# Seven block products in place of eight in the experts of two batches (attention and two expert layers, one core)

## The chip, the cores and the metric

The kernel runs on one core of a Trainium2 chip. The metric is the device time of one execution in microseconds. Engines: TensorE (PE, with its weight loads PEld), VectorE (DVE), ScalarE (ACT), GpSimd (POOL) and the DMA queues, here issued by SyncE (SP) and ACT.

## What is computed

```
attention: q, k, v of (4, 12, 448, 64)
  q_n, k_n = rmsnorm(q) * g_q, rmsnorm(k) * g_k
  attn = softmax(q_n @ k_n.T / 8);  o = attn @ v
x = o as (1792 tokens, 768)
first experts:   h = x @ w_in (768 x 2048);  g = where(h > 0, h, exp(h) - 1);  y = g @ w_out
second experts:  yn = y / rms(y) * rms_g
  g = yn @ w_gate (768 x 1536);  out = (silu(g) * (yn @ w_val)) @ w_out2
```

All inputs are float32. A product of two float32 matrices is made of three fp32r matmuls: each operand is split in a rounded part (h) and the rest (l), and wh·xh + wh·xl + wl·xh is summed (`mm3`, line 836). So each 128x128 weight tile costs three matmuls of 448 columns for each batch of 448 tokens.

## The kernel before, in words

Tokens lie on the free axis: a tile is 128 features x 448 tokens of one batch. The experts run in five stages (`STAGES`): first experts of batch 0, first experts of batch 1, second experts of batches 0 and 1, first experts of batches 2 and 3, second experts of batches 2 and 3. The attention of 24 head pairs is cut in pieces that are given between the steps of the first three stages; the last pairs end near the end of the third. From then on only the experts run.

First experts go in groups of NF1 = 4 chunks f of the 2048 hidden features: four `h_unit` steps (each output chunk f, for each batch: 6 weight tiles, 18 matmuls, then the ELU on ACT and DVE and the split of g in h and l), then six out steps in `acc_units` (each output chunk e, for each batch: 4 weight tiles, 12 matmuls), added up in the `ybig` tiles. Second experts go alike: four steps of gate and val, then six out2 steps. Here a batch pair makes 24 matmuls in each out step. With the last out group of the first experts each y is scaled and split for the second experts (`y_done`), and its squares are summed for the norm (`norm`), whose factor `rt` is multiplied to each gate product.

Weights are streamed in chunks of six tiles (`w_split`): read, split with `copy` and `tt` into one of 4 buffers of `r_w`, which hold them until TensorE has used them. At their first use they are converted (`w_convert`) and written back to `kept`; from the fourth stage on they are all read from `kept`. The attention outputs of batches 2 and 3 are spilled and read again at the end of the third stage, where `split_x` splits them.

Nothing is issued in the order in which the code is written. `plan.add` collects each operation with the engines that may do it and a price for each, and `Plan.schedule` deals them out in a list schedule with those prices; the earlier written goes first among those ready. `copy` may go to DVE, ACT or POOL (POOL not from a bank), `tt` to DVE or POOL (POOL only if both inputs are in SBUF). In the trace `copy` is on lines 327 to 333, `tt` on line 347 (DVE) and 349 (POOL), `stt` on line 364, `act` on line 372, matmuls on line 304.

```
def tt(dst, a, b, op, eng="vg"):
    ...
        alts["v"] = (c_tt(a, b, n), lambda: V.tensor_tensor(out=dst, in0=a, in1=b, op=op))
    if "g" in eng and two_sbuf(a, b):
        alts["g"] = (0.25 + 0.0022 * n, lambda: G.tensor_tensor(out=dst, in0=a, in1=b, op=op))
```

Of the kernel before, what the change touches and what calls it, by code (L numbers as in the profile page):

```python
# [19 lines left out]
P = 128  # L20
CW = 6
NF1 = 4
NF2 = 4
FIRST = 2
# [3 lines left out]
class Plan:  # L28
# [11 lines left out]
    def __init__(self):  # L40
        self.ops = []
        self.hist = {}
# [31 lines left out]
    def add(self, alts, outs, ins, lag=0.0, after=None, soon=False, dma=False):  # L74
# [3 lines left out]
        for aps, wr in ((ins, False), (outs, True)):  # L78
            for ap in aps:
                if ap is None:  # L80
                    continue
                name, hv, m = self.region(ap)
                h = self.hist.setdefault(name, [])
# [128 lines left out]
def k_tile_order(cd, cf1, cf2):  # L212

    order = []
    for f0 in range(0, cf1, NF1):
        for f in range(f0, f0 + NF1):
            order += [("in", c, f) for c in range(cd)]
        for e in range(cd):
            order += [("out", f, e) for f in range(f0, f0 + NF1)]
    for f0 in range(0, cf2, NF2):  # L220
# [3 lines left out]
        for e in range(cd):  # L224
            order += [("out2", f, e) for f in range(f0, f0 + NF2)]
# [4 lines left out]
def kernel(ctx: ExitStack, tc: tile.TileContext, dims, tok, qk, vr, gq, gk, wst, rmsg, ident_in, out):  # L230
# [8 lines left out]
    T, V, A, G, SP = nc.tensor, nc.vector, nc.scalar, nc.gpsimd, nc.sync  # L239
# [3 lines left out]
    plan = Plan()  # L243
# [174 lines left out]
    tks = [sb.tile([P, 15 * D], F32, name="tk"), wf[:, 0:15 * D]]  # L418
    tks += [yf[:, 7 * S:7 * S + 15 * D], yf[:, 12 * S - 15 * D:12 * S]]
    l_rw = Pair(sb.tile([P, 1024], F32, name="rw"), wf[:, 1024:2048])  # L420
    l_rb = Pair(sb.tile([P, 512], F32, name="rb"), wf[:, 2048:2560])
    l_qh = Pair(sb.tile([P, 1024], F32R, name="qh"), gf[:, 0:1024])
    l_ql = Pair(sb.tile([P, 1024], F32R, name="ql"), gf[:, 1024:2048])
    p_own = sb.tile([P, 3, 2 * S], F32, name="p")
    pt_own = sb.tile([P, 2, 3, S], F32, name="pt")
    l_p = Pair(p_own, tf[:, 0:6 * S].rearrange("p (a s) -> p a s", a=3))
    l_pj = Pair(sb.tile([P, S], F32, name="pj"), tf[:, 6 * S:7 * S])
    l_pt = Pair(pt_own, yf[:, 0:6 * S].rearrange("p (h k s) -> p h k s", h=2, k=3))
    l_pe = Pair(sb.tile([P, S], F32, name="pe"), yf[:, 6 * S:7 * S])
    r_rv = Ring("rv", 2, [P, 512])  # L430
# [7 lines left out]
    r_rsb = Ring("rsb", 2, [P, S])  # L438
    r_xf = Ring("xf", 1, [P, S])
    banks = [pp.tile([P, 512], F32, name=f"bank{k}") for k in range(8)]  # L440
# [13 lines left out]
    stream = [n for kind, _ in STAGES for n in (one if kind == 1 else two)]  # L454
# [7 lines left out]
    uses = {n: stream.count(n) for n in set(stream)}  # L462

    def w_split():
        i = wpos["spl"]
        n = stream[i]
        wpos["spl"] += 1
        if n in kept:
            c = r_wc.next()
            dma(c, kept[n], P * WN * 4)  # L470
        else:
            c = w_convert(n)
        w = r_w.next()
        copy(w[:, 0], c)
        tt(w[:, 1], c, w[:, 0], ALU.subtract)
        if n not in kept and uses[n] > 1:
            kept[n] = tc.dram_tile([P, WN], F32, name=f"kept{n}")
            dma(kept[n], c, P * WN * 4)
        spl_w[i] = w
# [37 lines left out]
    def w_ahead():  # L517
        while wpos["spl"] < min(wpos["i"] // CW + len(r_w.t), len(stream)):
            w_split()

# [358 lines left out]

    def h_unit(f, xs):  # L880
# [16 lines left out]
    def acc_units(bs, f0, nf, first, last, dst, half, done):  # L897
        for e in range(CD):
            w = take_w(nf)
            for b in bs:  # L900
                o = product(w, [gs[f0 + k, b] for k in range(nf)])
                if e == CD - 1:
# [21 lines left out]
    def first_experts(bs):  # L924
        xs = {b: [xT.pop(b * NPB + c) for c in range(CD)] for b in bs}
# [4 lines left out]

        def y_done(e, b, ye):
            g, sq = rg[:, e:e + 1], sqs[b]
            xh, xl = xslots.get(), xslots.get()
            act(xh, ye, AF.Copy, scale=g)
            stt(xl, ye, g, xh, ALU.mult, ALU.subtract)
            xns[b][e] = (xh, xl)
# [4 lines left out]
            yslots.put(ye)  # L941

        for f0 in range(0, CF1, NF1):
            last = f0 + NF1 >= CF1
            for f in range(f0, f0 + NF1):
                h_unit(f, xs)
                yield
            if last:
                for b in bs:
# [42 lines left out]
    def second_experts(bs):  # L992
# [6 lines left out]
        for f0 in range(0, CF2, NF2):  # L999
            last = f0 + NF2 >= CF2  # L1000
            for f in range(f0, f0 + NF2):
                yield from gv_unit(f, bs)
            if last:
                for b in bs:
# [29 lines left out]
    GOALS = [13.25, 19.75, 24, 24, 24]  # L1034
    phase(0)
# [3 lines left out]
    for s, (kind, bs) in enumerate(STAGES):  # L1039
# [13 lines left out]
        for step in first_experts(bs) if kind == 1 else second_experts(bs):  # L1053
# [102 lines left out]
```

## Time and profile before

| | |
|---|---|
| median of 3 runs | 1314.97 us (1314.67 to 1317.63) |
| profiled execution | 1316.42 us, span 1314.6 us |
| mean granted clock | 0.991 |
| TensorE busy | 1266.3 us, 96% of the span |
| POOL, DVE, ACT busy | 756.7, 650.2, 647.1 us |

The span is the time from the first to the last instruction; the execution's own time lies 1.8 us above it. Busy time is an average over stages that have different limits, so the views of single stretches say more than the table. Times of an engine include the time in which an instruction had begun and waited for a port.

### The profile page before, as it was taken

To read this page: it belongs to the slowest core of one execution; us is meant where nothing else is said; L and a number is where in the kernel's file an instruction comes from. 1 tells how busy PE (TensorE), PEld (TensorE's weight loads), DVE (VectorE), ACT (ScalarE), POOL (GpSimd) and SP (SyncE) were. 2 spreads that over 40 slices of the span, in tenths; PEclk is the share of its full clock that TensorE was granted. 3 is DMA by queue.
4 is the path that set the end of the run, shared out by engine and by line. 5 is a ranking of instruction groups with operands and counts; after the bars stand their busy time and mean duration, and the time that the engine had idled before them with its cause. 6 is when DMAs were issued, how large, how long until landed. Compare 5 with 4: busy or idle time off the path is not lost.

```text
span 1314.6 us, 17693 instructions
## 1 busy us (share of the span) xinstructions
PE 1266.3 (96%) x6484; PEld 1062.9 (81%) x6484; DVE 650.2 (49%) x1071; ACT 647.1 (49%) x1263; POOL 756.7 (58%) x576
## 2 busy tenths in 40 slices
PE   4899998988999999999999999999999999999998
PEld 3457766766777777888988889999999999999998
DVE  6787867796444569744564552102121652133332
ACT  5786767776665578555553541433323533221220
POOL 2385677776665588664653673645445765353450
PEclk8999999999999999999999999999999999999999
DMA  6477777665444354654445344111111111111112
GB/s 215 119 233 243 259 250 227 225 226 173 135 131 119 120 191 161 239 162 153 158 153 157 110 137 154 49 60 50 59 48 61 49 61 48 61 49 61 48 37 84
DMA packets 62487, 173.43 MB, mean 132 GB/s; under 512 B 10940, under 2 KB 20160, under 8 KB 62400
## 3 DMA queue, kind: packets, MB, share of 16 engines
q1 hardware_dynamic: 53760, 163.31, 38.3%
q10 hardware_dynamic: 8640, 8.99, 2.4%
q8 instruction: 51, 0.84, 0.3%
q14 instruction: 36, 0.29, 0.1%
HBM read 137.11 MB, written 35.17 MB: 131 GB/s over the span
## 4 chain that ended last, share of the span: by engine, by line
PE 79%; DMA 6%; POOL 5%; DVE 3%; ACT 3%; issue 2%; ACTq 0%; SPq 0%; POOLq 0%; DVEq 0%
PE bank L304 76%; PE bank L317 4%; POOL w L349 1%; DMA tk<-tok 1%; POOL ql L349 1%; DMA wr<-wst 1%; DMA rsum<-rt 1%; DMA rw<-qk 1%; DVE bank L660 1%; DMA wc<-kept 1%; POOL tbig L349 1%; POOL gbig L349 1%; ACT tbig L372 1%; DMA rsb<-rsum 1%; ACT p L372 1%
## 5 line engine op out<-in xcount | busy, mean ns | idle before, releaser
L304 PE MATMUL bank<-xs,w 128*128 128x448 f32 x2880 | 611.7, 369 | 4.3 <-POOL xs L349 2.8
L304 PEld LDWEIGHTS bank<-xs,w 128*128 128x128 f32 x2880 | 536.0, 189 | 55.1 <-issue 7.9
L304 PE MATMUL bank<-gbig,w 128*128 128x448 f32 x2016 | 434.8, 370 | 9.2 <-POOL gbig L349 4.3
L349 POOL TENSOR_TENSOR w<-wc,w 128x768 fp32r<-128x768 f32 x160 | 300.8, 1880 | 202.4 <-ACT w L329 196.0
L304 PEld LDWEIGHTS bank<-gbig,w 128*128 128x128 f32 x2016 | 373.8, 189 | 47.5 <-POOL gbig L349 6.4
L349 POOL TENSOR_TENSOR gbig<-tbig,gbig 128x448 fp32r<-128x448 f32 x107 | 132.0, 1234 | 68.6 <-ACT gbig L329 67.4
L329 ACT ACTIVATE w<-wc 128x768 fp32r<-128x768 f32 x91 | 76.9, 845 | 181.1 <-PE bank L304 173.2
L660 DVE TENSOR_REDUCE bank<-bank 128x1 f32<-128x448 f32 x168 | 98.6, 626 | 50.2 <-PE bank L304 49.4
L349 POOL TENSOR_TENSOR tbig<-tbig 128x448 f32<-128x448 f32 x67 | 85.0, 1269 | 64.7 <-DVE tbig L364 61.9
L364 DVE SCALAR_TENSOR_TENSOR tbig<-tbig,bank 128x448 f32<-128x448 f32 x64 | 39.5, 618 | 161.9 <-ACT tbig L372 161.9
L333 POOL TENSOR_SCALAR w<-wc 128x768 fp32r<-128x768 f32 x77 | 68.5, 890 | 84.0 <-PE bank L304 53.7
L364 DVE SCALAR_TENSOR_TENSOR wc<-wc,wt 128x768 int32<-128x768 int32 x68 | 86.8, 1276 | 29.3 <-ACT wc L495 24.5
L329 ACT ACTIVATE pt<-bank 128x384 f32<-128x384 f32 (+1 forms) x164 | 69.9, 448 | 61.2 <-PE bank L317 52.5
L372 ACT ACTIVATE p<-bank,nm,rr 128x448 f32<-128x448 f32 x126 | 90.2, 720 | 8.6 <-DVE nm L661 6.4
L329 ACT ACTIVATE gbig<-tbig 128x448 fp32r<-128x448 f32 x92 | 53.1, 577 | 78.9 <-DVE tbig L347 48.0
L372 ACT ACTIVATE tbig<-tbig 128x448 f32<-128x448 f32 x112 | 64.5, 576 | 47.4 <-DVE tbig L347 45.0
L347 DVE TENSOR_TENSOR tbig<-bank,tbig 128x448 f32<-128x448 f32 x48 | 29.9, 623 | 102.5 <-PE bank L304 102.3
L317 PE MATMUL bank<-ident,p 128*128 128x128 f32 x441 | 72.4, 280 | 7.8 <-DVE pt L327 3.2
L317 PEld LDWEIGHTS bank<-ident,p 128*128 128x128 f32 x441 | 54.5, 142 | 27.3 <-issue 4.9
L347 DVE TENSOR_TENSOR ybig<-bank,ybig 128x448 f32<-128x448 f32 x72 | 44.5, 620 | 62.2 <-PE bank L304 61.9
L364 DVE SCALAR_TENSOR_TENSOR ybig<-bank,ybig 128x448 f32<-128x448 f32 x48 | 30.0, 624 | 76.1 <-PE bank L304 76.1
L364 DVE SCALAR_TENSOR_TENSOR tbig<-tbig 128x448 f32<-128x448 f32 x48 | 52.9, 1102 | 24.0 <-ACT tbig L372 24.0
(103 smaller groups left out, 1197.5 us busy)
## 6 DMA issues: line engine op xcount, KB each, us to landing
wr<-wst SPq DMA_DIRECT2D x68, 768.0 KB
wc<-kept SPq DMA_DIRECT2D x100, 384.0 KB
kept<-wc SPq DMA_DIRECT2D x68, 384.0 KB
rw<-qk SPq DMA_DIRECT2D x21, 512.0 KB
tk<-tok SPq DMA_DIRECT2D x20, 480.0 KB
rv<-vr SPq DMA_DIRECT2D x24, 256.0 KB
out_t<-ybig SPq DMA_DIRECT2D x24, 224.0 KB
rb<-scr ACTq DMA_DIRECT2D x36, 128.0 KB
```

Source lines behind the costliest of these rows:

```text
L304: T.matmul(o, l, r, start=start, stop=stop)
L317: T.transpose(o, i, ident)
L329: alts["a"] = (c_a(n), lambda: A.activation(out=dst, in_=src, func=AF.Copy))
L333: lambda: G.tensor_scalar(out=dst, in0=src, scalar1=1.0, scalar2=0.0, op0=ALU.mult, op1=ALU.add),
L347: alts["v"] = (c_tt(a, b, n), lambda: V.tensor_tensor(out=dst, in0=a, in1=b, op=op))
L349: alts["g"] = (0.25 + 0.0022 * n, lambda: G.tensor_tensor(out=dst, in0=a, in1=b, op=op))
L364: {"v": (c_tt(a, b, size(dst)), lambda: V.scalar_tensor_tensor(out=dst, in0=a, scalar=s, in1=b, op0=op0, op1=op1))},
L372: {"a": (c_a(size(src)) + extra, lambda: A.activation(out=dst, in_=src, func=func, **kw))},
L660: vop(c_v1(S), lambda mx=mx, ot=o[t]: V.tensor_reduce(out=mx, in_=ot, axis=AX.X, op=ALU.max, negate=True), [mx], [o[t]])
```

## The change

In the last two stages (batches 2 and 3) the products of in, gate and val go by blocks (`quad`). A block has two output chunks f, two batches and the 6 input chunks as two halves of 3: a 2x2 times 2x2 product of blocks, done with seven products of 9 matmuls (`part`) in place of eight, by Strassen's scheme with fifteen sums: four of weights (`w_split`, 128x384 each, S1 to S4), four of inputs (`combo`, T1 to T4, 128x448 each) and seven of products (in `quad`, each with one operand in a bank). Each of the seven weight and seven input combinations is split in h and l. The input combinations of the first experts are made from the spilled tiles at the end of the third stage, those of the second experts in the last out group of the fourth, as soon as y for chunks c and c+3 of both batches is there: for that the out steps go in the order 0, 3, 1, 4, 2, 5 (`E_ORDER`, in all stages). The norm's squares and scale stay, the scale now writes y in place.

Once the attention has ended (`late`), its buffers are used again: as 18 more tiles for the input combinations (42 in all), as two more weight buffers (six chunks ahead instead of four; named `late` in the order), and as two more work tiles. The out products and all of batches 0 and 1 are as before. The core of the diff:

```diff
--- before.py
+++ after.py
+E_ORDER = (0, 3, 1, 4, 2, 5)
...
+    def again(t):
+        f = t if len(t.shape) == 2 else t.rearrange("p a s -> p (a s)") if len(t.shape) == 3 else t.rearrange("p h k s -> p (h k s)")
+        second[t.name] = {"t": None, "shape": list(t.shape), "name": f"late{len(second)}", "tag": t.name.rsplit("_", 1)[0]}
+        return f.bitcast(F32R)
...
+    for t in (p_own, pt_own):
+        f = again(t)
+        wide.append(f[:, 0:2 * WN].rearrange("p (a n) -> p a n", a=2))
+        spare += [f[:, 2 * WN + k * S:2 * WN + (k + 1) * S] for k in range(2)]
+    r_ws = Ring(tiles=[wf[:, k * WN:(k + 1) * WN] for k in range(2)])
+    r_th = Ring(tiles=[wf[:, 2 * WN + k * S:2 * WN + (k + 1) * S] for k in range(3)] + [r_wt.t[0][:, 0:S]])
+    r_more = [r_rsb.t[0], r_xf.t[0]]
...
+            for a, b in duos:
+                res += [("q", j, nums[k + a], nums[k + b]) for j in range(4)]
+            res += [("c", nums[k + nf + j]) for j in range(OG)]
...
+        if j == 0:
+            c0, c1 = w_f32(n0), w_f32(n1)
+            sa, sb = r_ws.next(), r_ws.next()
+            tt(sa[:, 0:HW], c1[:, 0:HW], c1[:, HW:WN], ALU.add)
+            tt(sa[:, HW:WN], sa[:, 0:HW], c0[:, 0:HW], ALU.subtract)
+            tt(sb[:, 0:HW], c0[:, 0:HW], c1[:, 0:HW], ALU.subtract)
+            tt(sb[:, HW:WN], c0[:, HW:WN], sa[:, HW:WN], ALU.subtract)
+            duo["c"] = (c0, sa, sb, c1[:, HW:WN])
+        spl_w[i] = split_w(duo["c"][j], HW if j == 3 else WN)
...
+    def part(w, x):
+        o = r_m.next()[:, 0:S]
+        for k in range(3):
+            mm3(o, w[k], x[k], k == 0, k == 2)
+        return o
+
+    TX = {}
+
+    def quad(eat):
+        w, tx = take_duo(), TX
+        u2, u3, u4, u7 = (r_tp.next() for _ in range(4))
+        p1 = r_tp.next()
+        copy(p1, part(w["A11"], tx["B11"]), "va")
+        p6 = part(w["S2"], tx["T2"])
+        tt(u2, p6, p1, ALU.add)
+        p2 = part(w["A12"], tx["B21"])
+        tt(p2, p2, p1, ALU.add)
+        eat(0, 0, p2)
+        p7 = part(w["S3"], tx["T3"])
+        tt(u3, p7, u2, ALU.add)
+        p5 = part(w["S1"], tx["T1"])
+        tt(u7, p5, u3, ALU.add)
+        tt(u4, p5, u2, ALU.add)
+        eat(1, 1, u7)
+        p4 = part(w["A22"], tx["T4"])
+        tt(p4, u3, p4, ALU.subtract)
+        eat(1, 0, p4)
+        p3 = part(w["S4"], tx["B22"])
+        tt(p3, p3, u4, ALU.add)
+        eat(0, 1, p3)
+        w_ahead()
+
+    def combo(c, x):
+        def sp(name, t):
+            h, l = xslots.get(), xslots.get()
+            copy(h, t)
+            tt(l, t, h, ALU.subtract)
+            TX.setdefault(name, [None] * 3)[c] = (h, l)
+
+        b11, b21, b12, b22 = x
+        t1, t2 = r_tp.next(), r_tp.next()
+        sp("B11", b11)
+        tt(t1, b12, b11, ALU.subtract)
+        tt(t2, b22, t1, ALU.subtract)
+        sp("T2", t2)
+        tt(b12, b22, b12, ALU.subtract)
+        sp("T3", b12)
+        sp("T1", t1)
+        sp("B21", b21)
+        tt(t2, t2, b21, ALU.subtract)
+        sp("T4", t2)
+        sp("B22", b22)
...
+    def h_quad(f, bs):
+        quad(lambda i, j, o: h_eat(f + i, bs[j], o))
...
+        quad(gate)
+        yield
+        quad(val)
+        yield
...
-        for e in range(CD):
+        for e in E_ORDER:
...
+            act(ye, ye, AF.Copy, scale=g)
+            if e >= 3 and b == bs[1]:
+                combo(e - 3, [y[k, bb] for bb in bs for k in (e - 3, e)])
...
+    def late():
+        state["late"] = True
+        for z in spare:
+            xslots.put(z)
+        r_w.t += wide
+        r_tp.t += r_more
...
             if step == "next":
-                if spilled:
-                    until(target(NPAIR) + 1)
-                    for b in ahead[1]:
-                        for i in range(b * NPB, b * NPB + NPB):
-                            xf = r_tp.next()
-                            dma(xf, xT[i], P * S * 4)
-                            split_x(i, xf)
+                if ahead is not None and ahead[0] == 1 and s + 1 in FAST:
+                    if not state:
+                        until(target(NPAIR) + 1)
+                        late()
+                    combos(ahead[1])
                 continue
```

`Engine` (new) hands each operation on to its engine and puts the reused tile in place of the old one; with it all instructions of the changed kernel carry the line 260.

The order of instructions is the same on every engine, but for buffer names, up to the first sum of input tiles in the third stage. From there on TensorE has 180 instructions fewer (6079 for 6259). Two places:

POOL, in the last out group of the first experts of batches 2 and 3 (`tbig` holds work tiles, `w` the split weights; `wc` weights, `wr` their sums, `ybig` y, `xs` and `late` the combinations). Before:

```order
L349 TENSOR_TENSOR w_97<-wc_93,w_97 128x768
L349 TENSOR_TENSOR tbig<-tbig 128x448 x4
L349 TENSOR_TENSOR w_98<-wc_94,w_98 128x768
L349 TENSOR_TENSOR tbig<-tbig 128x448
L333 TENSOR_SCALAR w_99<-wc_92 128x768
```

Now:

```order
L260 TENSOR_TENSOR xf_124<-ybig,rsb_122 128x448
L260 TENSOR_TENSOR xs_69<-rsb_122,xs_68 128x448
L260 TENSOR_TENSOR xs_81<-xf_124,xs_80 128x448
L260 TENSOR_TENSOR late_6535<-ybig,late_6535 128x448
L260 TENSOR_TENSOR w_97<-wc_93,w_97 128x384
L260 TENSOR_TENSOR xs_79<-ybig,xs_78 128x448
L260 TENSOR_TENSOR tbig<-tbig 128x448
L260 TENSOR_TENSOR wr<-wr,wc_94 128x384
L260 TENSOR_TENSOR tbig<-ybig,tbig 128x448
L260 TENSOR_TENSOR xs_83<-tbig,xs_82 128x448
```

Between two weight chunks stood sums of squares; now sums and splits of combinations and sums of weights stand there too, and most weight splits of this stretch have gone to DVE.

DVE, where the norm of these batches ends and the gate products begin (`bank` is PSUM, `gbig` takes the split squares and later g). Before:

```order
L347 TENSOR_TENSOR gbig<-tbig,gbig 128x448 x2
L380 RECIPROCAL tbig<-tbig 128x448
L347 TENSOR_TENSOR tbig<-bank_125,tbig 128x448
L380 RECIPROCAL tbig<-tbig 128x448
L364 SCALAR_TENSOR_TENSOR tbig<-tbig 128x448
L347 TENSOR_TENSOR tbig<-bank_126,tbig 128x448
L347 TENSOR_TENSOR tbig<-tbig,bank_127 128x448
```

Now:

```order
L260 TENSOR_TENSOR tbig<-tbig,ybig 128x448
L260 TENSOR_TENSOR gbig<-tbig,gbig 128x448
L260 TENSOR_TENSOR tbig<-bank_126,tbig 128x448
L260 RECIPROCAL tbig<-tbig 128x448 x2
L260 TENSOR_TENSOR bank_127<-bank_127,tbig 128x448
L260 TENSOR_TENSOR tbig<-bank_128,tbig 128x448
L260 TENSOR_TENSOR tbig<-bank_127,tbig 128x448
L260 TENSOR_TENSOR xf_124<-bank_129,tbig 128x448
L260 TENSOR_TENSOR rsb_122<-bank_129,tbig 128x448
L260 SCALAR_TENSOR_TENSOR wr<-wr,tbig 128x448
```

The two reciprocals stood one gate read apart; now both stand ahead of all but one of the reads of the first block's products, the one of the sixth product, and four of the five bank reads that follow are sums of the scheme.

## Rows read from the trace of the kernel before

**Rows 1.** Page, parts 1 and 2: busy time, and 40 slices of the span.

```profile
PE 1266.3 (96%) x6484; PEld 1062.9 (81%) x6484; DVE 650.2 (49%) x1071; ACT 647.1 (49%) x1263; POOL 756.7 (58%) x576
...
PE   4899998988999999999999999999999999999998
...
PEclk8999999999999999999999999999999999999999
```

**Rows 2.** Chain of waits, its last rows: start, duration (us), engine, tile, instructions.

```profile
773.84 7.30 PE bank L304 x36
781.47 529.64 PE bank L304 x2612
```

**Rows 3.** Windows: stretch, its length, busy us (instructions) of each engine, clock, DMA share.

```profile
core 0: us, PE busy (x) PEld busy (x) DVE busy (x) ACT busy (x) POOL busy (x), PEclk, DMA share, GB/s
200.00:300.00 100.00, 91.58 (x482) 70.15 (x481) 77.98 (x129) 71.71 (x156) 75.71 (x58) 0.97 0.67 223
...
814.00:1050.00 236.00, 236.00 (x1166) 218.70 (x1165) 53.70 (x81) 85.15 (x145) 125.38 (x95) 1.00 0.18 55
1050.00:1311.00 261.00, 261.00 (x1289) 241.66 (x1287) 81.45 (x100) 63.41 (x95) 119.77 (x85) 1.00 0.18 56
1019.70:1048.70 29.00, 29.00 (x145) 26.87 (x144) 17.91 (x24) 14.23 (x25) 22.23 (x17) 1.00 0.18 55
```

**Rows 4.** Groups by form, 814 to 1052 us: operation, count | busy us, mean ns.

```profile
L349 POOL TENSOR_TENSOR w<-wc,w 128x768 fp32r<-128x768 f32 x33 | 61.8, 1874 | 58.7 <-ACT w L329 57.2
L349 POOL TENSOR_TENSOR gbig<-tbig,gbig 128x448 fp32r<-128x448 f32 x32 | 37.0, 1155 | 41.8 <-ACT gbig L329 41.7
L347 DVE TENSOR_TENSOR ybig<-bank,ybig 128x448 f32<-128x448 f32 x36 | 22.5, 624 | 45.8 <-PE bank L304 45.7
...
L329 ACT ACTIVATE gbig<-tbig 128x448 fp32r<-128x448 f32 x33 | 19.1, 578 | 22.2 <-DVE tbig L364 22.1
L333 POOL TENSOR_SCALAR w<-wc 128x768 fp32r<-128x768 f32 x21 | 18.0, 859 | 12.3 <-PE bank L304 11.6 <-ACT tbig L372 0.7
...
L329 ACT ACTIVATE w<-wc 128x768 fp32r<-128x768 f32 x12 | 10.1, 846 | 54.2 <-PE bank L304 54.2
```

**Rows 5.** Groups by form of DVE, 1055 to 1310 us.

```profile
L364 DVE SCALAR_TENSOR_TENSOR tbig<-tbig 128x448 f32<-128x448 f32 x24 | 29.0, 1210 | 16.2 <-ACT tbig L372 16.2
...
L380 DVE RECIPROCAL tbig<-tbig 128x448 f32<-128x448 f32 x2 | 5.9, 2944 | 0.0
```

**Rows 6.** Timeline of DVE and of POOL, 1068 to 1084 us: start, duration, instruction.

```profile
1071.69 1.72 DVE L364 SCALAR_TENSOR_TENSOR tbig<-tbig 128x448 f32<-128x448 f32 x1 [0.70 <-ACT tbig L372]
...
1082.63 0.62 DVE L364 SCALAR_TENSOR_TENSOR tbig<-tbig 128x448 f32<-128x448 f32 x1 [0.70 <-ACT tbig L372]
...
1071.08 1.85 POOL L349 TENSOR_TENSOR w<-wc,w 128x768 fp32r<-128x768 f32 x1
```

**Rows 7.** Timeline, 638.5 to 641.6 us.

```profile
638.95 1.16 POOL L349 TENSOR_TENSOR tbig<-tbig 128x448 f32<-128x448 f32 x1 [0.56 <-DVE tbig L364]
...
639.36 1.56 DVE L364 SCALAR_TENSOR_TENSOR wc<-wc,wt 128x768 int32<-128x768 int32 x1 [0.49 <-ACT wc L495]
```

**Rows 8.** Timeline, 764 to 822 us: the tiles of batches 2 and 3 read again.

```profile
769.30 7.33 SPq L385 DMA_DIRECT2D tbig<-spill  x3
...
775.17 1.05 ACT L329 ACTIVATE xs<-tbig 128x448 fp32r<-128x448 f32 x2
...
794.92 0.57 POOL L333 TENSOR_SCALAR xs<-tbig 128x448 fp32r<-128x448 f32 x1 [1.53 <-DMA tbig<-spill]
795.57 1.15 POOL L349 TENSOR_TENSOR xs<-tbig,xs 128x448 fp32r<-128x448 f32 x1
```

**Rows 9.** The same timeline, where the first experts of batches 2 and 3 begin.

```profile
813.79 8.29 PEld L304 LDWEIGHTS bank<-xs,w 128*128 128x128 f32 x41
...
814.00 8.27 PE L304 MATMUL bank<-xs,w 128*128 128x448 f32 x40
```

**Rows 10.** Timeline, 1047 to 1062 us: the norm between first and second experts.

```profile
1052.93 0.56 PE L304 MATMUL bank<-gbig,ones 128*128 128x448 f32 x2
...
1054.44 2.95 DVE L380 RECIPROCAL tbig<-tbig 128x448 f32<-128x448 f32 x1
...
1058.04 2.94 DVE L380 RECIPROCAL tbig<-tbig 128x448 f32<-128x448 f32 x1
```

More of the change, by code (lines that the diff above doesn't have):

```diff
@@ L82, in add @@
                 name, hv, m = self.region(ap)
+                if name in self.second and ap.dtype == F32R:
+                    preds.update(rec[0] for rec in self.hist.get(name, []))
+                    name += "'"
                 h = self.hist.setdefault(name, [])
@@ L223, in k_tile_order @@
             order += [("val", c, f) for c in range(cd)]
-        for e in range(cd):
+        for e in E_ORDER:
             order += [("out2", f, e) for f in range(f0, f0 + NF2)]
@@ L457, with w_f32 @@
     kept = {}
[L462 to L467, printed above, removed]
+    uses = {}
+    for kind, _ in STAGES:
+        for n in one if kind == 1 else two:
+            uses[n] = uses.get(n, 0) + 1
+    def w_f32(n):
         if n in kept:
@@ new lines, in combos, with drop_combos, h_eat @@
+    def combos(bs):
+        for c in range(3):
+            x = []
+            for b in bs:
+                for k in (c, c + 3):
+                    x.append(r_tp.next())
+                    dma(x[-1], xT[b * NPB + k], P * S * 4)
+            combo(c, x)
+    def drop_combos():
+        for v in TX.values():
+            for x in v:
+                for z in x:
+                    xslots.put(z)
+        TX.clear()
+    def h_eat(f, b, o):
+        t1 = r_tp.next()
+        plan.add(
+            {
+                "v": (c_v1(S) if in_psum(o) else c_v2(S), lambda: V.tensor_scalar(out=t1, in0=o, scalar1=-1.0, scalar2=0.0, op0=ALU.mult, op1=ALU.max)),
+                "a": (c_a(S), lambda: A.activation(out=t1, in_=o, func=AF.Relu, scale=-1.0)),
+            },
+            [t1], [o],
+        )
+        act(t1, t1, AF.Exp, scale=-1.0)
+        stt(t1, t1, -1.0, o, ALU.add, ALU.max)
+        split_g((f, b), t1)
@@ L897, in acc_units @@
     def acc_units(bs, f0, nf, first, last, dst, half, done):
[L898 removed]
+        for e in E_ORDER:
             w = take_w(nf)
@@ L1000, in second_experts @@
             last = f0 + NF2 >= CF2
-            for f in range(f0, f0 + NF2):
-                yield from gv_unit(f, bs)
+            for f in range(f0, f0 + NF2, 2 if fast else 1):
+                yield from (gv_quad if fast else gv_unit)(f, bs)
             if last:
-                for b in bs:
+                drop_combos()
+                for b in bs if not fast else ():
                     for x in xns[b]:
@@ L1067 @@
         until(goal)
-        if kind == 1 and s + 1 < len(STAGES) and STAGES[s + 1][0] == 1:
-            norm(bs[0])
+        if kind == 1:
+            for b in bs:
+                norm(b)
     with tc.manual_schedule():
```

154 lines of the change are left out of this document (120 added, 34 removed).

## The prediction, made before the changed kernel ran

> **What bounds the kernel now.** I read the page's busy shares first: TensorE is busy for 96% of the span, POOL for 58%, DVE and ACT for 49% each, and the slices show where TensorE has its gaps: all in the first half, while the attention runs [rows 1]. The chain of waits says it more sharply. Its last link is one unbroken stretch of TensorE, 529.64 us with 2612 matmuls from 781.47 us to the end [rows 2]. That is 529.64 / 2612 = 0.2028 us a matmul and no wait at all. Everything that the change touches lies in this stretch, or in the few us ahead of it. So a matmul that goes away there is worth 0.2028 us, as long as the other engines keep up. The windows show how much room they have: from 814 to 1050 us (first experts of batches 2 and 3) POOL is busy 125.4 of 236 us, ACT 85.2, DVE 53.7; from 1050 to 1311 us (second experts) POOL 119.8 of 261, DVE 81.5, ACT 63.4 [rows 3].
>
> **The matmuls taken away.** Every 2x2 block of products (two output chunks f by two batches) took 4 products of 18 matmuls and now takes 7 of 9: 63 for 72. There are 8 such blocks in the first experts and 12 in the second, so 20 x 9 = 180 matmuls fewer; the order of instructions confirms it (6259 TensorE instructions before, 6079 after). Worth 180 x 0.2028 = **36.5 us**. Up to the first of the new sums the order is the same on every engine but for buffer names, so the first 770 us cost nothing more or less. DMA issues are 390 in both, and the DMA share in this part is 0.18 [rows 3]: nothing there.
>
> **What the sums cost, and where.** A DVE read of a bank costs 0.62 us whether it adds or not [rows 4]. A block has 7 such reads and one copy of the first product where 4 reads stood. That alone is about 2 us more of DVE in 12.8 us and fits. The price that matters is another one. DVE instructions with two SBUF inputs wait for POOL: alone such a 448-wide instruction takes 0.62 us, but one that started 0.61 us into a POOL instruction took 1.72 us and ended 0.48 us after it [rows 6]; a 768-wide one ended 0.81 us after the POOL instruction that it met [rows 7]. So I count POOL's instructions and these DVE ones **as one queue**: POOL 1.15 us for 448 columns, 1.85 for 768 [rows 4, 6], by their slope an estimate of 1.01 for 384; one-input ones 0.84 for 768 [rows 4], 0.57 for 448 [rows 8], some 0.50 for 384; DVE 0.48, 0.81, and 0.41 by the same slope. The Trainium skill ("SBUF — State Buffer", section "SBUF: two separate sides") says that this pair of ports is an exclusive lock, held for the whole instruction, and that the loser blocks entirely. By that the DVE price would be the whole 0.62 us, the queue some 5 us longer at the dearest place below, and the time 1312; the rows show 0.14 us of it hidden, and I go by them.
>
> Now the queue against TensorE, counted in the order of instructions, stage by stage.
>
> (a) *Combinations for the first experts*, made beside the last out group of batches 0 and 1. Before, 12 tiles were read again and split from about 775 to 796 us, and TensorE reached the first product that needs them at 814.0 us [rows 8, 9]: spare time of 18 us. Now 12 sums and 21 splits (12 before) must be done, with weight sums and splits between them. From the first sum to the last split the order has on POOL 24 x 1.15 + 4 x 1.01 + 1.85 + 0.57 = 34.1 us and on DVE 9 x 0.48 + 5 x 0.41 + 4 x 0.81 = 9.6 us: 43.7 us. In the trace the matmuls of that stretch run from about 778 to 814 us, 36 us. The queue is 7.7 us late; the first 15 matmuls (3 us) don't need the last tiles, so I take 4 us lost. Ends: 0 (the first block waits for nothing) and 8.
>
> (b) *The blocks of the first experts.* In a group of two blocks (126 matmuls, 25.6 us) POOL has 4 x 1.15 + 3 x 1.01 + 6 x 1.85 + 1.3 = 20.1 us, DVE 3 x 0.48 = 1.4: 21.5 of 25.6 us. It fits. ACT has 22 x 0.58 + 5 x 0.85 = 17 us [rows 4], fine. What is left is the handover to the out products, whose last input now comes through one more addition (0.62 us): 0.5 us in each of 4 groups, 2 us. Ends 0 and 8.
>
> (c) *The change from first to second experts*: the dearest place. y is combined as the last out group finishes it (steps 3, 4 and 5). From the end of step 3 to the end of the first gate and val blocks TensorE has 226 matmuls, 45.8 us. In the same stretch of the order the queue has 27 x 1.15 + 10 x 1.01 + 4 x 1.85 = 48.5 us of POOL and 24 x 0.48 + 3 x 0.81 = 13.9 us of DVE: 62.4 us. The next pair of blocks brings 6 x 1.15 + 5 x 1.01 + 6 x 1.85 = 23.1 and 9 x 0.48 + 0.81 = 5.1: 28.2 for 25.6 us. Together 90.6 for 71.4 us: the last split of this group comes 19 us late, and the out products need it. That TensorE runs partial products of the finished combinations meanwhile is inside the count. One us of out products can start ahead: I take 18 us lost. The norm adds no second cost: its two reciprocals of 2.9 us on DVE were there before [rows 5, 10], but now every read of a bank stands behind them. Ends: 8, if half of the lateness is weight work that could as well come later, and 26, if the queue has gaps while it waits for ACT.
>
> Before, the same stretch cost nothing: with 22.2 of 29 us of POOL busy in the last out group [rows 3], TensorE went on without a gap [rows 2].
>
> The Trainium skill ("GPSIMD Engine Reference", section "Engine selection") would have such additions on VectorE, as GpSimd takes about twice as long for two inputs. The rows agree (1.15 against 0.62). Had all 27 of POOL's 448-wide ones in (c) gone to DVE, the queue would be 27 x (1.15 - 0.48) = 18 us shorter and the loss nearly gone; the order doesn't do it.
>
> (d) *The two other groups of the second experts.* Four blocks: POOL 16 x 1.15 + 8 x 1.01 + 9 x 1.85 + 0.57 = 43.7, DVE 10 x 0.48 + 3 x 0.41 + 3 x 0.81 = 8.5: 52.2 for 252 matmuls, 51.1 us. Just full: 1 us late and 1 us for the handover, twice: 4 us. Ends 0 and 12.
>
> Sum: 36.5 - 4 - 2 - 18 - 4 = 8.5 us gained. The profiled execution took 1316.4 us (span 1314.6), 1.4 us above the median of the runs, 1314.97; 1316.4 - 8.5 = 1307.9, and by the median one us less: **1307 us**.
>
> **Rivals.**
>
> *The sums are hidden (faster).* The combinations of (c) are late, but what is late is mostly weight work for later; TensorE has 42 products of the first two combinations to run (8.5 us) and eight banks to run ahead in. For it speaks that each engine alone fits nearly everywhere (POOL 48.5 of 45.8 us in (c)) and that between 814 and 1311 us no wait stands in the chain [rows 2]. Then (a), (b) and (d) cost nothing and (c) 5 us: 1316.4 - 36.5 + 5 = 1285 us. Against it: POOL works in a fixed order, so what is written ahead of the last split is done ahead of it.
>
> *The queue doesn't run full (slower).* While attention and products ran together, from 200 to 300 us, POOL and DVE were each busy for three quarters of the time, and TensorE lost 8.4 of 100 us, with a granted clock of 0.97 [rows 3]. If the 20 blocks (20 x 12.8 = 256 us) go like that, because DVE stands in line behind POOL with bank reads behind it, they lose 21.5 us in place of the 6 of (b) and (d). With (a) at 8 and (c) at 24 us the sum is 36.5 - 53.5 = 17 us slower: 1333 us. It decides from a loss of 36.5 us on. Against it: from 814 us on the attention's own work on DVE and ACT is gone.
>
> *Even.* Losses of 33 to 41 us cancel the gain: within 4 us of before, which is what a measurement of this kernel can tell from no change (0.3%). It is simply the middle between forecast and slower rival.
>
> That the matmuls don't go away is excluded by the order.
>
> **How the numbers follow.** Forecast (1290 to 1311 us) 0.42, hidden 0.20, even 0.18, slower 0.20. Faster by over 0.3% is the first two, 0.60 with a little of their edges given to even; same 0.18; slower 0.22. The forecast's own range is 1290 to 1311. To hold 8 in 10 the range takes in most of both rivals: 1285 to 1329 us.
>
> **What would show it.** Right: the matmuls of the blocks still at 0.2028 us; TensorE idle for 12 to 24 us in all around the change from first to second experts, its waits ended by POOL's splits of the combinations or DVE's bank reads behind the reciprocals; POOL over 85% busy there, with DVE two-input instructions of 1.5 to 2 us; a smaller gap of up to 8 us at about 815 us; next to none within the first experts' groups. Wrong: gaps spread evenly over the 20 blocks (then the queue is not the place but the chain within a block), no gap at the change (then it is the first rival), or a granted clock at 1.2 GHz for long after a gap, which I price inside the ends of (c) only.

## The result and the profile after

The changed kernel takes **1294.72 us** (median of 4 runs, 1293.70 to 1302.74) against 1315.32 us for the kernel before in the same rounds. The ratio is 0.9854 with an interval of 0.9812 to 0.9895: 20.6 us or 1.5% faster, where the forecast said 1307 us. The time lies in the range that the forecast was given (1290 to 1311 us), on the side of the rival "the sums are hidden" (1285 us). A second set of runs gave 1297.60 against 1317.06 us, ratio 0.9868 (0.9838 to 0.9899).

The profiled execution took 1293.76 us, its span is 1292.0 us. Its page, busy times and slices, against [rows 1]:

```profile
PE 1238.1 (96%) x6304; PEld 1029.3 (80%) x6304; DVE 826.7 (64%) x1272; ACT 701.2 (54%) x1364; POOL 889.7 (69%) x666
...
PE   4999998997999999999999999999999989999998
...
DVE  6786876897453559763654548616354898388592
...
POOL 2485778777665588763744559958475999799590
PEclk9999999999999999999999999999999999999999
```

TensorE has 180 matmuls fewer. POOL rises from 58% to 69%, DVE from 49% to 64%, and around the 33rd slice, where both are full, lies what TensorE loses in the second half. The chain of waits, longest pieces from 793 us on, answers to [rows 2]:

```profile
793.26 1.87 POOL tbig L260
799.20 3.68 DMA xf<-spill
806.76 195.60 PE bank L260 x951
1008.79 2.52 DVE late L260
...
1068.51 2.20 POOL w L260
...
1100.17 188.00 PE bank L260 x918
```

The one stretch of 529.64 us has become two, 195.60 and 188.00 us long. Between them, for 98 us, the chain is made of short pieces, 35.8 us of them on POOL and 34.0 on DVE: the change from the first to the second experts.

The windows, columns as in [rows 3]: the end of the last out group of batches 0 and 1; then the first experts from their first product on; then the first gate and val blocks of the second experts with their out group (400 matmuls).

```profile
805.00:811.70 6.70, 5.86 (x29) 5.10 (x28) 6.65 (x8) 2.67 (x5) 6.70 (x6) 1.00 0.61 196
...
811.70:1033.80 222.10, 222.10 (x1082) 202.80 (x1081) 117.33 (x152) 105.19 (x185) 158.86 (x118) 1.00 0.19 58
...
1033.80:1126.20 92.40, 86.08 (x401) 74.87 (x400) 71.87 (x78) 44.11 (x74) 85.58 (x60) 0.98 0.19 56
```

In the last row TensorE needs 92.4 us for 400 x 0.2028 = 81.1 us of matmuls: **11.3 us lost**. In what follows this is called the loss at the change, and always worked out so. In the first row TensorE has a gap of 0.84 us; in the second there is no gap at all. What TensorE waits for from 1030 us on (us in total, times, longest):

```profile
PE bank L260 <- DVE ybig L260: 2.2, 2, 1.8
PE bank L260 <- POOL qh L260: 1.7, 1, 1.7
PE bank L260 <- DVE late L260: 1.6, 1, 1.6
PE bank L260 <- DVE tbig L260: 0.3, 1, 0.3
PE bank L260 <- POOL late L260: 0.3, 1, 0.3
```

Late reads of y's banks take 2.2 us, splits of combinations (`qh`, and here `late`) 3.6. All these waits lie between 1036 and 1063 us; the out products behind the blocks, from 1096.3 us on, wait for 0.1 us in all. So 6.3 of the 11.3 us are gaps. In the rest TensorE counts as busy with matmuls that start further apart than 0.2028 us: those next to each gap, and those at a lower clock (last section).

How the full engines look there: POOL and DVE, timeline (start, duration, instruction).

```profile
1031.73 1.53 POOL L260 TENSOR_TENSOR tbig<-ybig,tbig 128x448 f32<-128x448 f32 x1
1033.23 1.54 POOL L260 TENSOR_TENSOR xs<-tbig,xs 128x448 fp32r<-128x448 f32 x1
1034.73 1.53 POOL L260 TENSOR_TENSOR late<-tbig,late 128x448 fp32r<-128x448 f32 x1
1036.23 1.51 POOL L260 TENSOR_TENSOR xs<-ybig,xs 128x448 fp32r<-128x448 f32 x1
...
1058.20 1.16 POOL L260 TENSOR_TENSOR ql<-tbig,ql 128x448 fp32r<-128x448 f32 x1
```

```profile
1032.17 1.58 DVE L260 TENSOR_TENSOR ybig<-ybig 128x448 f32<-128x448 f32 x1
1033.67 1.58 DVE L260 TENSOR_TENSOR late<-ybig,late 128x448 fp32r<-128x448 f32 x1
1035.17 1.57 DVE L260 TENSOR_TENSOR xs<-ybig,xs 128x448 fp32r<-128x448 f32 x1
1036.67 1.55 DVE L260 TENSOR_TENSOR tbig<-tbig,ybig 128x448 f32<-128x448 f32 x1
1038.14 1.14 DVE L260 TENSOR_TENSOR ybig<-bank,ybig 128x448 f32<-128x448 f32 x2
```

They take turns. While both have such work, one 448-wide instruction of each ends every 1.50 us: POOL's 1.15 us and 0.35 us for DVE's. Both engines' durations hold the wait for the other, so their busy shares say less than the count of instructions. The split that ends last (POOL, 1058.20 us) ends at 1059.4 us, 25.6 us after the last product of the first experts (1033.8 us).

### The profile page after: what moved, and what is told of

Read it like the earlier page. It is cut to its first block, busy times and chain, and to the rows that moved or that the text cites. A ratio compares the mean times of both kernels' runs of the same rounds, so it can differ in the third digit from the quotient of the medians.

```text
span 1292.0 us, 17836 instructions
## 1 busy us (share of the span) xinstructions
PE 1238.1 (96%) x6304; PEld 1029.3 (80%) x6304; DVE 826.7 (64%) x1272; ACT 701.2 (54%) x1364; POOL 889.7 (69%) x666
## 4 chain that ended last, share of the span: by engine, by line
PE 72%; POOL 7%; DMA 7%; DVE 6%; ACT 3%; issue 3%; ACTq 0%; SPq 0%; POOLq 0%; DVEq 0%
PE bank L260 72%; POOL w L260 2%; DMA tk<-tok 1%; DMA rw<-qk 1%; POOL tbig L260 1%; POOL gbig L260 1%; POOL ql L260 1%; DMA wr<-wst 1%; ACT tbig L260 1%; POOL wr L260 1%; DVE tbig L260 1%; DVE ybig L260 1%; DMA wc<-kept 1%; DMA rsum<-rt 1%; DVE bank L260 1%
## 5 line engine op out<-in xcount | busy, mean ns | idle before, releaser
L260 PE MATMUL bank<-xs,w 128*128 128x448 f32 x1872 | 421.1, 371 | 5.7 <-DVE tbig L260 2.9
L260 PEld LDWEIGHTS bank<-xs,w 128*128 128x128 f32 x1872 | 346.6, 189 | 42.4 <-issue 7.9
L260 POOL TENSOR_TENSOR w<-wc,w 128x768 fp32r<-128x768 f32 (+1 forms) x129 | 241.8, 1876 | 98.8 <-ACT w L260 95.1
L260 ACT ACTIVATE w<-wc 128x768 fp32r<-128x768 f32 (+1 forms) x89 | 71.4, 802 | 90.9 <-PE bank L260 79.6
L260 POOL TENSOR_TENSOR gbig<-tbig,gbig 128x448 fp32r<-128x448 f32 x72 | 94.2, 1311 | 18.2 <-ACT gbig L260 16.8
L260 DVE SCALAR_TENSOR_TENSOR wc<-wc,wt 128x768 int32<-128x768 int32 x68 | 87.2, 1282 | 29.2 <-ACT wc L260 24.5
L260 POOL TENSOR_SCALAR w<-wc 128x768 fp32r<-128x768 f32 (+1 forms) x59 | 52.9, 898 | 69.7 <-PE bank L260 49.0
L260 PE MATMUL bank<-xs,late 128*128 128x448 f32 x288 | 69.5, 369 | 2.4 <-DVE ybig L260 2.2
L260 PE MATMUL bank<-late,w 128*128 128x448 f32 x252 | 64.7, 369 | 0.0
L260 POOL TENSOR_TENSOR ql<-rw,qh 128x512 fp32r<-128x512 f32 x35 | 50.5, 1454 | 18.3 <-ACT qh L260 17.8
L260 DVE TENSOR_SCALAR wt<-wr 128x768 uint16<-128x768 uint16 x68 | 62.3, 916 | 0.3
```

The lines of the kernel that those rows point to most:

```text
L260: return lambda *a, **k: f(*[real(x) for x in a], **{n: real(x) for n, x in k.items()})
```

## The experiments

The loss at the change is the largest, so most runs ask what it consists of. A table of all runs stands at the end of this section.

**Weight work off POOL.** In the first four blocks of the second experts the low half of each weight tile is a copy on ACT:

```
-        tt(w[:, 1, 0:k], src, w[:, 0, 0:k], ALU.subtract)
+        if low:
+            tt(w[:, 1, 0:k], src, w[:, 0, 0:k], ALU.subtract)
+        else:
+            copy(w[:, 1, 0:k], src, "a")
...
-        spl_w[i] = split_w(duo["c"][j], HW if j == 3 else WN)
+        spl_w[i] = split_w(duo["c"][j], HW if j == 3 else WN, n0 < N1 or n0 >= N1 + 2 * NF2)
```

> For the eight weight tile groups of the first four pairs of blocks of the second experts, the low half of the split is a plain copy on ACT in place of a subtraction on POOL or DVE (so the low halves are not the remainders, and the output is not the reference's). The combinations themselves, their chain and the reciprocals stay as they are. In the order, the queue of POOL and two-input DVE work from the end of the fourth output step to the end of the first gate and val blocks falls by some 13 us. Theory (one queue for POOL and DVE's two-input instructions, and the weight work in it delays the combinations): of the 10.6 us that TensorE lost from 1034 to 1096 us most goes, at most 3 us stay, and the kernel is 8 to 10 us faster than the changed kernel, near 1285 us. Rival (the loss is the latency of the chain y, scale, sums, splits, products of the last combination and of the norm): the loss stays at 9 to 11 us and the time near 1294 us.

The window from the first gate product on:

```profile
1038.40:1128.90 90.50, 85.66 (x401) 76.48 (x400) 62.62 (x70) 48.87 (x81) 67.44 (x52) 0.96 0.19 57
```

POOL is busy for 18 us less (67.4 for 85.6), yet the loss is 90.5 - 81.1 = 9.4 us, only 1.9 us less. The theory as it was put, the whole queue to the end of the first blocks, falls: at most 3 us should have stayed. Some 8 of the 13 us of weight work stand behind the last split of the combinations in the order, and what stands behind it holds up little. So the theory was narrowed: what counts is the queue **ahead of that last split**. The times decide less than the loss: the ratio, 0.9821 (0.9779 to 0.9862), can't be told from that of the changed kernel, and the profiled execution is the slowest of four.

**Sums off POOL.** From the combinations for the first experts of batches 2 and 3 on (`state` is set there), POOL may do no 448-wide sum or split and no copy:

```
-        if "g" in eng and two_sbuf(a, b):
+        if "g" in eng and two_sbuf(a, b) and not (state and n == S):
...
-        if "g" in eng and not ps:
+        if "g" in eng and not ps and not state:
```

> From the first experts of batches 2 and 3 on, the planner may not give POOL any 448-wide sum nor any copy of a split: these go to DVE and ACT. In the order the queue count for the same stretch falls from 85 to 67 us, for 66.5 us of matmuls, while DVE's own work there rises from 56 to 68 us. Theory (shared queue): TensorE's loss between 1034 and 1096 us falls from 10.6 us to 2 to 5 us and the kernel is 5 to 9 us faster than the changed one, 1286 to 1290 us. Rival (DVE, busy without a break there, is the bound by its own instructions, and POOL does not hold it up): DVE has 12 us more to do, the loss grows to 15 us or more, 1300 us or slower.

Windows from the first gate product on:

```profile
1044.00:1060.00 16.00, 10.38 (x34) 8.28 (x33) 13.86 (x21) 10.69 (x19) 4.34 (x3) 0.68 0.00 1
1060.00:1080.00 20.00, 16.14 (x63) 13.31 (x63) 17.16 (x17) 8.62 (x15) 8.79 (x6) 0.83 0.07 20
...
1044.00:1151.10 107.10, 91.57 (x401) 79.59 (x400) 79.82 (x102) 47.67 (x78) 53.71 (x35) 0.90 0.15 45
```

The loss grows to 26.0 us, the rival's case, and the kernel is no faster than before (ratio 0.9992, 0.9967 to 1.0016). POOL is busy for 4.3 of the first 16 us, while DVE has a sum every 0.53 us and the reads of the banks stand in the same row. Timeline of DVE:

```profile
1052.01 0.61 DVE L261 TENSOR_TENSOR xs<-ybig,xs 128x448 fp32r<-128x448 f32 x1
1052.54 0.61 DVE L261 TENSOR_TENSOR ybig<-bank,ybig 128x448 f32<-128x448 f32 x1
1053.08 0.61 DVE L261 TENSOR_TENSOR xs<-tbig,xs 128x448 fp32r<-128x448 f32 x1
```

The read of y's bank at 1052.54 us comes 8.5 us after the last product had ended, and three more follow it, the last at 1056.12 us. So the shared queue is one bound, DVE's own row is the other, and the planner's mixture lies between them.

**Half of the change.** FAST = (3,) and FAST = (4,), with the plain tiles made where they are needed.

> Seven block products only in the first experts of batches 2 and 3; the second experts run eight, as before, so no combinations are made at the change to them. 72 matmuls fewer, 14.6 us. Theory: 1.1 us lost at 806 us and no gap at the change; the matmul rhythm of 0.2067 us, where it stands, takes up to 3 us: about 10.5 us faster than before, and 3.4 us more if the lead that the changed kernel had at 770 us is real: 1301 to 1305 us. Rival (the loss at 1034 to 1096 us comes from the norm and the last y's, not from the combinations): the gap stays with 6 us or more, 1308 us or slower.

> Seven block products only in the second experts of batches 2 and 3; the first experts take the plain tiles, as before. 108 matmuls fewer, 21.9 us. Theory: the combinations at the change are as many as in the changed kernel and cost the same 10 to 12 us; the other groups 1 to 2 us: 8 to 11 us faster than before (11 to 14 with the lead at 770 us), 1301 to 1307 us. Rival (the first experts' blocks push weight work into the change, and without them the queue is empty when it begins): the loss there falls under 5 us, 1297 us or faster.

```profile
1041.00:1129.50 88.50, 88.50 (x438) 81.91 (x437) 29.30 (x32) 29.58 (x46) 44.96 (x33) 1.00 0.19 58
```

```profile
1044.70:1137.50 92.80, 84.56 (x402) 74.13 (x401) 69.94 (x77) 41.58 (x67) 84.07 (x60) 1.00 0.19 56
```

In the first window (first experts alone) 436 matmuls take 88.5 us, 0.1 us over 436 x 0.2028: norm and last y's alone, in the order of the kernel before, cost nothing. In the second the loss is 92.8 - 81.1 = 11.7 us, as in the whole change: the blocks of the first experts push nothing into it. (Some 2 us of it are waits from 1109 us on, behind the blocks.) Both theories held; the combinations for the second experts make the loss. The medians are 1304.75 and 1307.46 us, the first within its range, the second half a us above.

**Shorter queue ahead of the last split.** The squares of y are added up on TensorE:

```
-            z = r_tp.next() if e else sq
-            act(z, ye, AF.Square)
-            if e:
-                tt(sq, sq, z, ALU.add)
+            z = xslots.get()
+            act(z, ye, AF.Square)
+            block([(held[b][:, 0:S], ones, z, e == E_ORDER[0], e == E_ORDER[-1])], 0.205)
+            xslots.put(z)
...
```

The norm then reads the two banks that were held for it.

> The sums of squares for the norm of batches 2 and 3 are no longer added up by ten 448-wide additions on POOL and DVE: ACT writes each square rounded, and TensorE adds them up against the matrix of ones in two banks that are held for it (12 matmuls in place of 4, 1.6 us more). So about 9 us of two-input work leave the queue ahead of the last combination; the combinations, their chain and the weight work stay. Theory (what stands in the queue ahead of the last combination's last split is what TensorE waits for): the loss between the last out group of the first experts and the end of the first gate and val blocks falls from 10.6 us to 2 to 5 us, the time by 4 to 7 us against the changed kernel, 1287 to 1291 us. Rival (the last combination's own chain alone sets the loss): it stays at 9 us or more, 1295 to 1298 us with the matmuls added.

```profile
1039.80:1125.20 85.40, 82.92 (x398) 73.81 (x397) 63.03 (x70) 39.95 (x65) 77.09 (x54) 1.00 0.19 61
```

What TensorE waits for there:

```profile
PE bank L260 <- DVE gbig L260: 1.4, 1, 1.4
PE bank L260 <- DVE tbig L260: 0.4, 1, 0.4
PE bank L260 <- POOL qh L260: 0.4, 1, 0.4
PE bank L260 <- POOL late L260: 0.3, 1, 0.3
```

396 matmuls, 80.3 us: 5.1 us lost, 6.2 less, at the upper end of what the theory gave (2 to 5). The time, 1292.20 us, lies 1.2 us above its range. Of the 5.8 us of waits for late reads and splits of combinations 0.4 are left (`qh`); the longest wait is now for a split of g at 1099 us, behind the blocks. POOL has 77 of 85 us to do, 10 more than in the run with weight work taken away, and TensorE loses 4 us less: it is not the whole work that counts. A rival, that the gain comes from the norm, which ends earlier here too, finds little room: in the changed kernel TensorE waits for 0.3 us behind the reciprocals.

**Same queue, last y's first.** The planner ranks the additions that read y's banks ahead of older work:

```
+                    plan.early = 200 if last and bs == (2, 3) else 0
                     tt(dst[e, b], o, dst[e, b], ALU.add)
+                    plan.early = 0
...
```

> In the last out group of the first experts the additions that read y's banks get ahead of the older sums in the planner's order, so that the last two y's are read as their products end (in the changed kernel 8.5 us later, behind DVE sums that wait for POOL). Nothing is taken out of the queue. Theory (one queue, its whole work ahead of the last split counts): the other combinations come later in exchange, the loss stays at 9 to 12 us, 1292 to 1297 us. Rival (the late reads of the last y's set the loss): it falls by 4 to 8 us, 1286 to 1290 us.

Timeline of DVE; the last product ended at 1036.4 us:

```profile
1035.38 0.61 DVE L263 TENSOR_TENSOR ybig<-bank,ybig 128x448 f32<-128x448 f32 x1
1035.91 1.04 DVE L263 TENSOR_TENSOR ybig<-ybig 128x448 f32<-128x448 f32 x1
1036.88 0.61 DVE L263 TENSOR_TENSOR ybig<-bank,ybig 128x448 f32<-128x448 f32 x1
```

The last y is read at 1036.88 us, at once, where the changed kernel had its last product done at 1033.8 and read it at 1042.3. The loss is 12.9 us all the same: no wait is for a read of y's banks now, and 4.9 us are for POOL's splits. The rival falls: the late reads are a symptom of the queue. The time, 1300.15 us, is 3 us above what either expected.

**Four weight tiles** in place of six (the line `r_w.t += wide` taken out), and the output steps in plain order (E_ORDER = (0, 1, 2, 3, 4, 5)):

> The weight ring stays at four tiles in the seven block stages. A block of seven products uses all four, so the next block's second tile can only be split once five of the seven products are done. Theory: the split of a tile takes 0.85 + 1.85 us and the waits between them, about 3 us, while TensorE has 3.7 us of products left and then one product of the next block: 1 to 2 us lost in each of most of the 20 blocks, 15 to 35 us in all, 1308 to 1328 us. Rival (four tiles are enough, since the sums of the weights are made ahead in tiles of their own): within 4 us of the changed kernel. On the side: if the slower spacing of the matmuls (0.2067 in place of 0.2027 us) hangs on the two added tiles, it is gone here.

> The output steps run 0 to 5 in order again, so that the first combination can begin after the fourth step of the last out group instead of the second. Theory (one queue): the same work stands in a shorter time, with the queue idle before it; the loss at the change grows from 10.6 to 14 to 18 us, 1297 to 1303 us. Rival (only the last combination's chain counts, and it begins at the same step): the loss stays at 9 to 12 us, 1292 to 1297 us.

```profile
816.80:1038.00 221.20, 221.20 (x1081) 202.76 (x1080) 114.60 (x147) 100.67 (x173) 161.98 (x127) 1.00 0.19 60
1038.00:1137.30 99.30, 89.14 (x401) 77.62 (x401) 73.76 (x80) 46.36 (x78) 88.81 (x64) 0.95 0.15 48
```

With four tiles the first experts run without a gap (first row): my expectation of 1 to 2 us in each block was wrong. Neither expectation named what was seen: the added tiles are worth 6 to 7 us at one place, the change, where the loss is 99.3 - 81.1 = 18.2 us and the longest of TensorE's waits (us in total, times, longest) is for POOL's split of a weight tile:

```profile
PE bank L260 <- POOL w L260: 3.9, 2, 3.4
```

The plain order loses 13.3 us there, between the two expectations. Two profiles of the changed kernel give 11.3 and 12.3 us, so a difference of 1 to 2 us settles nothing.

**Beside each other, in five rounds:** the changed kernel, the version with the squares on TensorE, and that version with the last y's first.

> The changed kernel as it is, on the same chip and in the same rounds as the next two. Every theory: the gain against before is 1.3 to 1.7%; the loss between the last out group of the first experts and the end of the next out group 11 to 12 us again; the time at which TensorE has done its first 3800 matmuls, where the program is still that of before, lies anywhere between 764 and 772 us, as in the profiles so far, so the 3.4 us lead of the first profile is no effect of the change.

> The version with the sums of squares on TensorE, directly beside the changed kernel. Theory (one queue): 6 us less loss at the change for 1.6 us of added matmuls, so 4 to 5 us faster than the changed kernel in the same rounds, a ratio to before lower by 0.003 to 0.004. Rival (the difference of the first look is chance): within 1.5 us.

> The sums of squares on TensorE and the last y's read first, together. Theory (one queue, its order matters little): within 2 us of the version with the squares alone, the loss at the change 4 to 6 us. Rival (with the queue shorter, the late reads become the bound): 2 us or more faster than it, the loss under 3 us.

The squares on TensorE gain 1297.60 - 1291.48 = 6.1 us on the changed kernel, where 4 to 5 were expected (ratios 0.9868, 0.9838 to 0.9899, and 0.9807, 0.9778 to 0.9837). Both together take **1289.90 us**, ratio 0.9802 (0.9776 to 0.9827): the fastest version here, but not to be told from the squares alone, although the loss falls from 5.1 to 3.0 us. That lies between the two expectations: with the queue shorter, the order may matter a little.

The queue count of the prediction, done again with what the timelines showed: POOL's instructions as before, DVE's two-input ones at 0.37 us (0.35 by the alternation above; 0.33 and 0.75 for 384 and 768 columns), from the end of the third output step (1018.9 us in the changed kernel) up to the last split in the order. The last column is what of the loss lies in matmuls without a gap, beyond 0.2028 us each, while the granted clock was at 1.2 GHz.

| kernel | median us | ratio to before | queue counted | its end, counted | measured | after last product | loss at the change | of it at 1.2 GHz |
|---|---|---|---|---|---|---|---|---|
| changed | 1294.72 | 0.9854 | 38.6 | 1057.5 | 1059.4 | 25.6 | 11.3 | 1.1 |
| changed_again | 1297.60 | 0.9868 | 38.6 | - | - | 25.5 | 12.3 | 3.0 |
| weights_low_on_act | 1294.18 | 0.9821 | 33.6 | 1057.1 | 1058.9 | 20.5 | 9.4 | 2.3 |
| squares_on_pe | 1292.20 | 0.9826 | 32.4 | 1056.2 | 1057.8 | 18.0 | 5.1 | 0 |
| squares_again | 1291.48 | 0.9807 | 32.4 | - | - | 18.0 | 5.1 | 0 |
| squares_and_y_first | 1289.90 | 0.9802 | 31.9 | 1053.3 | 1052.8 | 15.5 | 3.0 | 0 |
| y_first | 1300.15 | 0.9880 | 37.6 | 1059.1 | 1061.2 | 24.8 | 12.9 | 3.3 |
| plain_e_order | 1298.32 | 0.9873 | 39.3 | 1059.3 | 1059.4 | 24.5 | 13.3 | 3.3 |
| four_tiles | 1303.74 | 0.9915 | 36.1 | 1059.3 | 1060.7 | 22.7 | 18.2 | 4.2 |
| sums_on_dve | 1314.98 | 0.9992 | 24.6 | 1053.7 | 1070.7 | 26.7 | 26.0 | 6.8 |
| first_only | 1304.75 | 0.9911 | - | - | - | - | 0.1 | 0 |
| second_only | 1307.46 | 0.9942 | - | - | - | 24.5 | 11.7 | 0 |

The counted end is within 2.1 us of the measured one in all but sums_on_dve, where DVE's own row runs 17 us longer than the queue. Summed over the instructions that the traces show in that stretch, from the end of the third step to the last split, the same prices give 41.0 us in the changed kernel and an end within 0.7 us of the measured one in the same seven: POOL and DVE together had hardly an idle moment there.

The loss goes with the end of the split in part only. In weights_low_on_act the split ends 5 us sooner and 2 us come of it; in squares_on_pe it ends 8 us sooner and 6 come of it. TensorE's waits lie on the way to that split, and why the first of the two runs gains so little is open; part of it is the clock, 2.3 us for 1.1. Without the last column y_first (9.6) and plain_e_order (10.0) are level with the two profiles of the changed kernel (10.2 and 9.3). In four_tiles the loss is larger than the split explains, since weight tiles come late as well.

## Why the prediction was right, and where its sum was off

The direction, the main place and the range were right. The size was not: the gain was 20 us where the sum said 8.5, and the time lies 12 us from the forecast. Step by step, from the profiled executions:

- **36.5 us of matmuls taken away**: held; 6484 to 6304 records, at 0.2028 us.
- **"The first 770 us cost nothing more or less"**: TensorE had done its first 3800 matmuls at 767.6 us before and at 764.2 after, 3.4 us ahead. The other profiles of kernels with the same order up to there have 764.8 to 771.8 us. So that lead is no effect of the change that these runs could show, and it is part of the 22.6 us between the two spans.
- **(a) 4 us at the first combinations**: 1.1 us. The count was right: 7.7 us late was forecast, and the last split ended at 818.9 us, 7.1 us after the first product of the block (811.7). What failed is "the first 15 matmuls don't need the last tiles, so I take 4 us lost": the tiles come in the order in which the seven products use them, and the last ones are wanted by the sixth and seventh product only. The 0.84 us that are seen are a wait for DVE's read of a bank, at 806 us, 5 us ahead of the place forecast.
- **(b) 2 us at handovers**: there is no gap at any of the four handovers. 3.1 us are lost all the same, by another cause (last section). The sum was nearly right by luck, the reason wrong.
- **(c) 18 us at the change**: 11.3 us, within the ends of 8 and 26. This term was the main one mis-sized. The place, POOL without an idle us from 1034 to 1090, and DVE instructions of 1.5 to 2 us are as forecast. Too dear was DVE's price: 0.48 us, read from single encounters [rows 6], where in steady alternation it is 0.35 us; over the 24 instructions of the count that makes 24 x 0.13 = 3 us. Wrong also was which products wait: "the last split of this group comes 19 us late, and the out products need it". The out products waited for 0.1 us; what waited were the gate and val products, for the splits of their own combinations and for banks, at 1036 to 1063 us. As in (a), what comes late in the queue is wanted late. The reciprocals [rows 10], which I placed ahead of every bank read, cost 0.3 us of waiting; in first_only, where they stand as before, nothing.
- **(d) 4 us in the other groups**: 1.2 us, without a gap.
- **"Had all 27 of POOL's 448-wide ones in (c) gone to DVE, ... the loss nearly gone"**: wrong, and shown so by sums_on_dve. I had counted the shared queue alone and not DVE's own row, in which the reads of the banks stand.

Sum: 1.1 + 3.1 + 11.3 + 1.2 = 16.7 us lost of 36.5, where 28 were forecast. Without the lead of 3.4 us the spans differ by 19.2 us, so 17.3 were lost; 0.6 have no place here.

Of the signs that the prediction named, POOL was busy for over 85% at the change (85.6 of 92.4 us) and nothing was lost in gaps within the first experts' groups. TensorE's gaps there come to 6.3 us, though, not 12 to 24, the blocks' matmuls were not all at 0.2028 us, and the gap at about 815 us is missing.

Of the rivals, "the sums are hidden" was right about (a), (b) and (d) having next to no gap and about TensorE running ahead, but put 5 us where 11.3 were lost. "The queue doesn't run full" fell: DVE behind POOL with bank reads behind it cost nothing in the blocks of the first experts. "Even" needed a loss of 33 us.

On the two rules: the Trainium skill ("SBUF — State Buffer", section "SBUF: two separate sides") has POOL and DVE take turns for whole instructions. They do take turns, but a pair takes 1.50 us where 1.15 + 0.62 = 1.77 would follow. Some 0.13 us of that are records that overlap: by their starts, instructions of one engine that don't wait for the other lie 1.11 us (POOL, squares_on_pe from 1051.12 us on) and 0.53 us (DVE, sums_on_dve) apart, which makes 1.64. The Trainium skill's advice to prefer VectorE for such additions ("GPSIMD Engine Reference", section "Engine selection") agrees with the durations (0.61 against 1.15 us), but following it with all of them cost the whole gain here (ratio 0.9992 for 0.9854).

## What to carry to other kernels

Where a planner's engines are full, don't weigh the whole work of a stage against TensorE: count the queue up to the last thing that TensorE can't do without, and ask in which order it uses what arrives late. Some 6 us of queue taken out ahead of that point gave 6 us here; some 13 us of weight work, 5 of them ahead of it, gave 2 in the one profile there is. So the place in the queue matters, but one count of it doesn't give the loss. Before moving sums from one engine to another, count the other one's row too, with the bank reads in it; the cheapest place tried for ten additions was TensorE itself, the engine that waited, with 8 more matmuls (1.6 us).

## What was not expected

**Two spacings of the matmuls at the same clock.** Of the same out group of the first experts, 144 matmuls, before and after:

```profile
843.20:872.40 29.20, 29.20 (x146) 27.06 (x145) 0.62 (x1) 9.35 (x16) 10.41 (x8) 1.00 0.18 54
```

```profile
837.40:867.20 29.80, 29.80 (x146) 27.05 (x146) 7.79 (x7) 11.34 (x21) 17.03 (x13) 1.00 0.19 54
```

The granted clock is 1.00 in both, TensorE has no gap in either, and yet the starts lie 0.2027 us apart in the first and 0.2067 us in the second. In the kernel before the longer spacing doesn't hold anywhere from 781 us on. In the changed one it sets in within a seven product block, lasts over the out group that follows and ends some way into the next block. That is 3.1 us in the first experts (222.1 us for 1080 matmuls, 219.0 at 0.2028) and about 1.2 us in the second. It doesn't hang on the two added tiles (four_tiles has it too), and with the plain products of second_only the first experts are free of it. Its cause is open.

**The clock after short gaps.** Windows of the changed kernel:

```profile
1036.00:1040.00 4.00, 1.90 (x9) 1.41 (x9) 4.00 (x5) 1.72 (x4) 4.00 (x4) 1.00 0.00 0
1040.00:1044.00 4.00, 3.58 (x12) 2.70 (x11) 4.00 (x5) 2.61 (x6) 4.00 (x4) 0.57 0.13 18
1044.00:1048.00 4.00, 2.76 (x14) 2.21 (x12) 4.00 (x3) 3.29 (x8) 4.00 (x4) 1.00 0.20 81
```

After a stretch in which TensorE was busy for 1.9 of 4 us, the granted clock is 0.57, near the level of 1.2 GHz, and back at 2.4 GHz in the next one, although TensorE had a gap there as well. Matmuls that start more than 0.208 us apart without a gap make up 3.1 us of the loss at the change, those after each short wait among them; 1.1 us of this lie in the stretch at 1.2 GHz. In the second profile of the changed kernel the clock was low twice (0.96 over the window, for 0.98), and 3.0 of 12.3 us were lost so. In second_only a wait of 2.6 us left it at 1.00. I had put the clock inside the ends of (c); it is between a tenth and a quarter of that term.
